# Six more warm-up matmuls on TensorE ahead of a fused attention, FFT-filter and gate kernel

## The chip, the cores and the metric

The kernel runs on one core of one Trainium2 chip. The metric is the device time of one execution in microseconds (us). The kernel before takes 237.54 us (median of three runs, 237.5 to 238.29). Two times are compared as after / before.

A core has five engines that run side by side: TensorE (PE, matmuls; its weight loads are shown apart as PEld), VectorE (DVE), ScalarE (ACT), GpSimd (POOL), and SyncE (SP), which here issues nearly all the transfers (DMAs). Matmuls write into PSUM, which has eight banks here, and another engine copies the result out.

## The reference: what is computed

Three results on the same input `x` of 2048 tokens x 640, in bf16:

```
a = attention with 32 heads of 20, in 4 segments of 512 tokens,
    plus a linear memory (M, z) carried from segment to segment, then @ wo
b = irfft2( rfft2(x) * (w_r + 1j*w_i) )
g = sigmoid( sum(x * gate_w) )
out = g * a + (1 - g) * b
```

Within a segment, q, k and v are `x @ wq`, `x @ wk` and `x @ wv`; the scores are masked with a causal mask and go through a softmax; the memory is read with `phi(q)` and updated with `phi(k)`. What is changed below computes nothing of this: it works on zeros, and nothing reads its result.

## The kernel before, in words

**A recorded program and a planner.** The class `Kern` doesn't write instructions directly. Its methods (`warm_up`, `loads`, `consts`, `project`, `attend`, `fft` and so on, called from `record`, line 860) record operations, each with the buffers that it reads and writes, a planned cost, and the engines that could run it. A group of matmuls is one operation (`mms`, line 544); its planned cost is the sum over its matmuls of `max(columns / 2.4 + 2.8, 25.4)` ns in the mode that the warm-up uses (lines 499 and 547), and it notes two instructions for each matmul, a weight load and the matmul (`op.count`, line 564).

**The order is written out by hand.** `ORDER` (line 633) lists every operation as 2 x its number plus the choice of engine. `Sched.schedule` (line 117) turns it into one queue for each engine and then plays the queues forward in planned time. In that play it settles what is left open:

- which PSUM bank a group of matmuls gets: the one among the allowed ones that comes free first in planned time (`place`, line 159). Groups of the pool "gen" share banks 4 to 7, the scores have 0 to 3;
- which semaphore a transfer gets, and which earlier transfer it must wait for, so that no more than about 1.6 MB is under way (`window`, line 169);
[...]
- when TensorE's code is expected to be there, in blocks of 256 instructions (lines 199 to 203 and 240 to 248).

`emit` (line 290) then writes the waits and the instructions.

**The start.** VectorE clears a tile `G` (line 852), and ten groups of one matmul each multiply zeros into one bank of the pool "gen" (`warm_up`, line 847; `NWARM`, line 858). Each has a 128 x 128 weight and 512 columns and is entered with 1000 columns for the planned cost. They stand first in TensorE's queue. Meanwhile SyncE and ScalarE issue the loads: the first columns of `wq` and `wk`, three transposing loads of the first segment of `x` into `xT` (`xt_load`, line 923), then parts of `xsb` (the same `x` in the order that the FFT wants), the rest of `wk`, `beta`, `fcat` (a table), `wv`, and the rest of `wq`.

**What follows on TensorE.** `proj_direct` (line 1017) computes q and k of the first eight heads straight into the padded layout `qkp`: twenty groups, each four column tiles of 32 wide, which need `xT` and the first columns of `wq` and `wk`. ScalarE and VectorE copy the four results out of PSUM (line 573 on VectorE, 571 on ScalarE), the first scores start from them, and the exponentials (line 1319) start from the scores. Then come the other tiles of k (`proj_tile`, line 1083, which need the rest of `wk`), the first transforms of the FFT on `xsb` once VectorE and GpSimd have folded it (`fold`, line 946), the tiles of v, and the other tiles of q. The projected q and k of the other heads go through a buffer `qk_scr` in the chip's memory and come back as `qkp`. From there on attention, memory and FFT run interleaved to the end.

In the trace all matmuls have line 561 (559 where a weight is split in four), so they are told apart by their tiles; the warm-up's are `psum<-G`.

Of the kernel before, what the change touches and what calls it, by code (L numbers as in the profile page):

```python
# [12 lines left out]
P = 128  # L13
# [5 lines left out]
L = 512  # L19
# [485 lines left out]
class Kern:  # L505
# [10 lines left out]
    def b(self, *key):  # L516
        v = self.bufs.get(key)
        if v is None:
            v = self.bufs[key] = Buf(str(key))
        return v  # L520
# [326 lines left out]
    def warm_up(self):  # L847

        self.Sc.group += 1
        b = self.b  # L850
        t = self.G
        self.one("dve", lambda e: e.memset(t.ap(0, [1, 640]), 0.0), 320, [], [b("warm")], -2.0, name="warm")
        bank = Bank(1, "gen")
        for k in range(self.NWARM):
            self.mms([(lambda k=k: (self.ps(bank, 0, [1, L]), t.ap(0, [1, P]), t.ap(P, [1, L]), True, True, {}), 1000)],
                     [b("warm"), bank], [], -1.0, name="warm")

    NWARM = 10

# [804 lines left out]
```

## Time and profile before

| what | value |
|---|---|
| median of three runs | 237.54 us (237.5 to 238.29) |
| the profiled execution: span from the first to the last instruction | 238.5 us |
| the profiled execution's own time outside the span | not shown; the span is all that is known of it |
| instructions | 10359 |
| busy: PE / DVE / ACT / POOL | 224.9 / 194.8 / 197.1 / 162.0 us |
| the same as shares of the span | 94% / 82% / 83% / 68% |
| mean granted TensorE clock | 0.993 |
| busy share of PE in the windows 0 to 13.5 us and 13.5 to 40 us | 10.23 of 13.50, 26.23 of 26.50 us |

How to read it: a row of the timeline has a start, a duration, an engine, a line of the kernel, and what is written from what; in square brackets stands how long the engine was idle before, and what released it ("issue" when nothing in the profile explains it). Ends of matmuls are modelled, so starts are the safer reading: the distance between the starts of two matmuls of one kind is the pace. The granted clock is a fraction of TensorE's full clock. A chain is the work followed back from the last instruction, at each step to what released it.

### The profile page before, as it was taken

The page shows a single profiled execution, that of the slowest core. Times are in us where ns is not written, and L with a number is a line of the kernel's source. Part 1 is how long each engine was busy: PE and PEld are TensorE (multiplying, and loading weights), DVE is VectorE, ACT ScalarE, POOL GpSimd, SP SyncE. Part 2 cuts the span into 40 slices and gives each one's busy share as a digit, 9 for nine tenths or more (in the row PEclk, how much of TensorE's full clock was granted, in tenths as well). Part 3 has the DMA queues.
Part 4 walks back from the last instruction along what each step waited for, and adds up shares of the span by engine and source line. Part 5 has one row for each costly group of instructions (what it writes and reads, how often), then busy time and mean ns, then how long its engine had stood idle before and what let it go on. Part 6 is the DMA issues. An engine that isn't in the chain of part 4 may idle for free.

```text
span 238.5 us, 10359 instructions
## 1 busy us (share of the span) xinstructions
PE 224.9 (94%) x4391; PEld 142.1 (60%) x4391; DVE 194.8 (82%) x486; ACT 197.1 (83%) x233; POOL 162.0 (68%) x300
## 2 busy tenths in 40 slices
PE   6899999979999999999989999899999999989994
PEld 2576566656546666555657665456554456657794
DVE  0189998859999998899998888999999996847453
ACT  2079888969999998999989999988999888788820
POOL 8133139436769976737888979777998677786840
PEclk9799999999999999999999999999999999999999
DMA  7999659997879586493886683544998767492224
GB/s 148 294 330 271 196 148 171 231 230 157 230 181 231 156 214 184 122 269 100 179 230 186 182 278 87 174 124 138 200 273 210 187 142 109 95 82 85 74 70 110
DMA packets 59121, 42.18 MB, mean 177 GB/s; under 512 B 30212, under 2 KB 55364, under 8 KB 59076
## 3 DMA queue, kind: packets, MB, share of 16 engines
q1 hardware_dynamic: 58036, 40.96, 71.8%
q8 instruction: 34, 0.56, 1.0%
q10 hardware_dynamic: 1040, 0.57, 0.9%
q14 instruction: 11, 0.09, 0.1%
HBM read 23.32 MB, written 12.30 MB: 149 GB/s over the span
## 4 chain that ended last, share of the span: by engine, by line
PE 62%; ACT 13%; DMA 11%; DVE 9%; issue 2%; POOL 1%; SPq 1%; DVEq 0%; POOLq 0%
PE psum L561 54%; ACT ex L1319 11%; PE psum L559 8%; DMA qkp<-qk_scr 3%; DVE Pt L1496 2%; DMA u_scr<-ub 2%; DMA pkn<-phk 2%; DMA xT<-in_A_x_dram 2%; DMA tt<-tab_tt 2%; POOL ex L1340 1%; DMA dnc<-u_scr 1%; DVE qu L573 1%; SPq L594 1%; DVE Bt L573 1%; DVE phk L1141 1%
## 5 line engine op out<-in xcount | busy, mean ns | idle before, releaser
L1319 ACT ACTIVATE ex<-psum 128x2048 bf16<-128x2048 f32 (+4 forms) x92 | 138.5, 1506 | 13.2 <-PE psum L561 10.9
L1340 POOL TENSOR_SCALAR_AFFINE_SELECT ex<-ex 128x256 bf16<-128x256 bf16 (+2 forms) x224 | 118.6, 551 | 29.5 <-ACT ex L1319 6.1
L561 PE MATMUL psum<-qkp 20*64 20x64 bf16 (+5 forms) x1280 | 32.3, 270 | 3.5 <-ACT ex L1319 2.8
L561 PE MATMUL psum<-xT,wq 128*128 128x512 bf16 (+1 forms) x135 | 31.7, 423 | 2.3 <-DMA xT<-in_A_x_dram 2.0
L561 PE MATMUL psum<-xT,wk 128*128 128x256 bf16 (+1 forms) x280 | 32.6, 282 | 1.3 <-issue 1.3
L561 PEld LDWEIGHTS psum<-qkp 20*64 20x64 bf16 x1280 | 13.3, 103 | 21.9 <-ACT ex L1319 16.3
L1496 DVE TENSOR_TENSOR Pt<-psum,Wt 128x642 bf16<-128x642 f32 x32 | 25.4, 818 | 1.1 <-PE psum L561 0.9
L561 PE MATMUL psum<-wv,xT 128*32 128x321 bf16 (+3 forms) x390 | 26.1, 301 | 0.0
L561 PEld LDWEIGHTS psum<-xT,wk 128*128 128x128 bf16 (+1 forms) x280 | 20.5, 101 | 7.8 <-issue 4.0
L961 POOL TENSOR_TENSOR xsb<-xf 128x320 bf16<-128x320 bf16 (+2 forms) x11 | 8.1, 744 | 20.5 <-DVE xf L956 11.3
L559 PE MATMUL psum<-wo,oU 128*32 128x320 bf16 x480 | 21.5, 300 | 0.0
L573 DVE CAST ot<-psum 128x320 bf16<-128x320 f32 x22 | 10.4, 488 | 10.3 <-PE psum L559 7.2
L1171 DVE TENSOR_TENSOR va<-psum,ebx 128x320 bf16<-128x320 f32 x32 | 15.2, 487 | 4.2 <-PE psum L561 2.7
L561 PE MATMUL psum<-big,Cp 128*128 128x321 bf16 (+1 forms) x96 | 18.0, 302 | 0.2
L561 PEld LDWEIGHTS psum<-wv,xT 128*32 128x32 bf16 (+1 forms) x390 | 14.1, 96 | 6.3 <-issue 0.9
L561 PE MATMUL psum<-ex,va 128*32 128x64 bf16 (+3 forms) x576 | 17.6, 257 | 0.2
L561 PE MATMUL psum<-big,Ac 128*128 128x161 bf16 (+2 forms) x96 | 17.8, 256 | 0.0
L573 DVE CAST Bt<-psum 128x322 bf16<-128x322 f32 x28 | 14.3, 520 | 2.5 <-PE psum L561 2.3
L561 PEld LDWEIGHTS psum<-ex,va 128*32 128x32 bf16 x576 | 10.9, 96 | 8.7 <-POOL ex L1340 1.8
L561 PE MATMUL psum<-tt,Yt 128*128 128x256 bf16 (+1 forms) x96 | 15.8, 275 | 0.3 <-DVE Yt L1501 0.3
L1542 DVE TENSOR_TENSOR G<-eo,psum 128x320 bf16<-128x320 f32 x32 | 14.9, 477 | 1.2 <-ACT eo L571 0.5
L561 PEld LDWEIGHTS psum<-xT,wq 128*128 128x128 bf16 (+1 forms) x135 | 9.8, 105 | 10.2 <-DMA xT<-in_A_x_dram 2.5
(98 smaller groups left out, 392.0 us busy)
## 6 DMA issues: line engine op xcount, KB each, us to landing
qkp<-qk_scr SPq DMA_DIRECT2D x28, 160.0 KB
tt<-tab_tt SPq DMA_DIRECT2D x8, 512.0 KB, 4.5
qk_scr<-qu SPq DMA_DIRECT2D x12, 256.0 KB, 2.8
u_scr<-ub SPq DMA_DIRECT2D x12, 256.0 KB, 3.1
xsb<-in_A_x_dram SPq DMA_DIRECT2D x8, 320.0 KB, 5.0
oU<-u_scr SPq DMA_DIRECT2D x15, 128.0 KB, 3.6
out_dram<-ot SPq DMA_DIRECT2D x12, 160.0 KB
Wt<-in_B_w_r_dram SPq DMA_DIRECT2D x16, 80.2 KB, 4.7
```

The lines of the kernel that those rows point to most:

```text
L559: h = e.matmul(dst, wt, r_, start=st, stop=sp_, **{**kw, "tile_position": (0, q), "skip_group_check": True})
L561: h = e.matmul(o_, l_, r_, start=st, stop=sp_, **kw)
L573: alts["dve"] = (lambda e: e.tensor_copy(dst(), src()), 67 + 1.04 * n, 68.0)
L594: return e.dma_start_transpose(d_, s_)
L961: self.either(lambda e, dst=dst, src=src, d0=d0, n=n, op=op: e.tensor_tensor(xs.ap(o + dst, [D, 2], [1, n]), xf.ap(src + d0, [321, 2], [1, ...
L1141: fmin = lambda e: e.tensor_tensor(dst(), dst(), et.ap(0, [1, L]), ALU.min)
L1171: self.one("dve", lambda e: e.tensor_tensor(va.ap(i * H * VW + h0 * VW, [VW, nh], [1, DH]), self.ps(bank, 0, [DH, nh], [1, DH]), self.ebx. ...
L1319: self.one("act", lambda e, d=d, q=q: e.activation(self.ex.ap(*d), self.ps(bank, *q), ACT.Exp, scale=SC), n, [bank], [self.exb(s, 2 * pr + ...
L1340: self.one("pool", lambda e: e.affine_select(self.ex.ap(e0 + d0, [1280, 4], [1, n], np_=np_), self.ex.ap(e0 + s0, [1280, 4], [1, n], np_=np_),
L1496: self.one("dve", lambda e, ri=ri, Pt=Pt, Wt=Wt, wo_=wo_, bank=bank: e.tensor_tensor(Pt.ap(ri * 322, [644, 2], [1, KD]), self.ps(bank, 0, ...
L1542: self.one("dve", lambda e, q=q, n2=n2, bank=bank, eo=eo: e.tensor_tensor(self.G.ap(n2 * D + 639 * q, [1 - 2 * q, 320]), eo.ap(q, [1, 320] ...
```

## The change

Groups 0 to 3 of the ten warm-up groups keep their one matmul. Groups 4 to 9 hold the same matmul twice. So TensorE gets 16 instead of 10 matmuls on zeros, all into the same bank. The number of operations stays the same, and so the numbers in `ORDER` still fit. The planned cost of a doubled group is twice that of a single one, and its count of instructions is 4 instead of 2, so the planner plays the rest of the program from a later planned time of TensorE.

```diff
         for k in range(self.NWARM):
-            self.mms([(lambda k=k: (self.ps(bank, 0, [1, L]), t.ap(0, [1, P]), t.ap(P, [1, L]), True, True, {}), 1000)],
-                     [b("warm"), bank], [], -1.0, name="warm")
+            warm = lambda: (self.ps(bank, 0, [1, L]), t.ap(0, [1, P]), t.ap(P, [1, L]), True, True, {})
+            self.mms([(warm, 1000)] * (1 if k < 4 else 2), [b("warm"), bank], [], -1.0, name="warm")
```

## The prediction

> **What bounds the kernel now.** I read the page first: how busy each engine is, the forty slices, and the chain that ended last. Then came the pieces of that chain in order of time, the busy time by stretches, and the timeline of the first 14 us. On the page:
> ```profile
> span 238.5 us, 10359 instructions
> ...
> PEclk9799999999999999999999999999999999999999
> ...
> PE 62%; ACT 13%; DMA 11%; DVE 9%; issue 2%; POOL 1%; SPq 1%; DVEq 0%; POOLq 0%
> ```
> TensorE carries 62% of the chain. In the second slice (6 to 12 us) the granted clock reads 0.7, the only low place in the whole row. The warm-up sits just ahead of it. The chain of the first 60 us:
> ```profile
> 6.94 29.51 PE psum L561 x425
> ...
> 37.86 0.69 DVE Ac L573
> ...
> 39.69 6.23 DMA qkp<-qk_scr
> ...
> 45.96 4.84 PE psum L561 x113
> 50.80 1.30 issue
> ```
> From 6.94 on TensorE is the chain for 29.5 us without a break, so what TensorE saves early there, the chain saves. Now the clock, in stretches of 3.41 us (why 3.41, below), and two short stretches at its edges:
> ```profile
> 0.63:4.04 3.41, 2.74 (x7) 1.00 0.62 145
> 4.04:7.45 3.41, 1.44 (x21) 1.00 1.12 206
> 7.45:10.87 3.42, 3.42 (x48) 0.50 0.94 307
> ...
> 48.41:51.82 3.41, 2.40 (x55) 1.00 1.11 228
> ```
> ```profile
> 7.40:7.60 0.20, 0.20 (x12) 0.64 0.49 141
> ...
> 10.80:11.00 0.20, 0.20 (x12) 0.83 1.19 365
> ```
> Columns: length, TensorE's busy time (matmuls), granted clock, DMA share, GB/s. A mean of 0.64 in 7.40 to 7.60 puts the drop to one half at 7.46; a mean of 0.83 in 10.80 to 11.00 puts the return at 10.87. The drop lasts 3.41 us. I therefore cut the time into stretches of that length, ending at those two edges. The stretch ahead of the drop was busy 1.44 of 3.41 us (42%). The stretch ahead of the return was full. The one ending at 51.82 was busy 70% and lost nothing.
>
> The matmuls show both clocks:
> ```profile
> L561 PE MATMUL psum<-G x10: 379/620/634, 1.3 to 4.6; 128*128 128x512 bf16 x10
> ```
> ```profile
> 1.30 3.67 PE L561 MATMUL psum<-G 128*128 128x512 bf16 x10 [1.30 <-DVE G L852]
> 6.94 0.40 PE L561 MATMUL psum<-xT,wq 128*32 128x512 bf16 x4 [1.97 <-DMA xT<-in_A_x_dram]
> 7.16 0.39 PE L561 MATMUL psum<-xT,wk 128*32 128x256 bf16 x8
> 7.73 0.66 PE L561 MATMUL psum<-xT,wk 128*32 128x256 bf16 x8
> 8.16 1.08 PE L561 MATMUL psum<-xT,wq 128*32 128x512 bf16 x8
> ...
> 13.08 0.43 PE L561 MATMUL psum<-qkp 20*64 20x512 bf16 x12
> 13.44 3.23 PE L561 MATMUL psum<-xT,wk 128*128 128x256 bf16 x28
> ```
> Groups of real work start 0.22 us apart at 6.94 and 7.16, then 0.43 apart at 7.73 and 8.16: half speed. The ten warm-up matmuls end at 4.97, and 1.97 us of idleness follow. Most of the warm-up went at half speed too, although the clock column reads 1.00 there (nothing is recorded before the first change). Its weight loads show it:
> ```profile
> 3.83 0.15 PEld L561 LDWEIGHTS psum<-G 128*128 128x128 bf16 x1 [0.28 <-issue]
> 4.16 0.31 PEld L561 LDWEIGHTS psum<-G 128*128 128x128 bf16 x2 [0.17 <-issue]
> ```
> Ten matmuls from 1.30 with the last start at 4.6 are 0.37 us apart in the mean, but the loads at 3.83 and 4.16 only 0.33, and the two at 4.16 closer still; so the clock rose near 4.04, the end of a stretch that was busy 2.74 of 3.41 us (80%).
>
> **The change, part by part.** Against the profiled execution: its span is 238.5 us, which is 0.96 above the median of the runs (237.54) and 0.21 above the highest (238.29). Its own time outside the span isn't shown, so I take differences from the span and apply them to the median.
>
> *Six more matmuls.* A full-clock matmul of 512 columns costs, by this row,
> ```profile
> 22.42 3.84 PE L561 MATMUL psum<-xT,wq 128*128 128x512 bf16 x17
> ```
> (3.84 - 0.38) / 16 = 0.216 us, the 0.38 being the tail of the last. Six cost 1.30 us and end at 4.97 + 1.30 = 6.27, ahead of 6.94, where the load xT releases the first real matmul. They cost nothing while the load covers them. Without a rise of the clock at 4.04 they would start 0.43 us apart as at 7.73 and 8.16, take 2.6 us, end at 7.5, and delay the real work by 0.6.
>
> *The clock.* The stretch from 4.04 to 7.45 gets 1.44 + 1.30 = 2.74 us of work, 80%: exactly the share at which the first stretch raised the clock, and above the 70% that kept it. So I expect no drop. Between 7.46 and 10.87 TensorE was full at half clock, and 3.41 x 0.5 = **1.71 us** go.
>
> [...]
>
> *What is late next.* Three things.
> ```profile
> 9.67 1.03 DVE L956 TENSOR_TENSOR xf<-xsb 128x640 bf16<-128x640 bf16 x2 [8.43 <-DMA xsb<-in_A_x_dram]
> 11.73 0.38 SPq L596 DMA_DIRECT2D wq<-in_A_wq_dram  x1
> 12.11 1.94 DVE L573 CAST qkp<-psum 128x512 bf16<-128x512 f32 x3 [1.41 <-PE psum L561]
> 13.07 0.16 PEld L561 LDWEIGHTS psum<-qkp 20*64 20x64 bf16 x12 [0.42 <-DVE qkp L573]
> ```
> ```profile
> SPq L596 <- DMA wk<-in_A_wk_dram: 1.6, 1, 1.6
> ```
> (1) VectorE's first cast would be wanted at 12.11 - 1.71 = 10.40, but two folds hold that engine until 10.70; the first scores behind it then come 0 to 0.3 us later than their 11.37; I take 0.1, since the first of three casts still ends at 10.70 + 0.65 = 11.35. (2) SyncE's issue at 11.73 waited 1.6 us for the second part of wk, so that part landed at about 11.7; the first tile that needs it would start at 13.44 - 1.71 + 0.1 = 11.83, with 0.1 to spare: 0. (3) From there to 37.86 the chain is TensorE, and then VectorE, SyncE, and the 6.23 us of a load. All of them follow TensorE, but stages of the remaining 200 us can give some back. Bounds: loss 0 to 1.6; I take 0.2, because the rows that I have of the next 25 us are of TensorE, not of loads.
>
> *The plan.* The queues keep their written order. But the planner charges each matmul 1000 columns, 1000 / 2.4 + 2.8 = 419.5 ns, so its warm-up is 6 x 0.42 = 2.5 us longer, while the chip's is 1.30 longer and hidden. PSUM banks, semaphores and the waits between VectorE and GpSimd are chosen from these planned times, and some will differ. The nearest row for a badly placed bank:
> ```profile
> PEld psum L561 <- ACT ex L1319: 16.6, 50, 0.9
> ```
> 0.33 us each. I bound this between two such waits fewer (-0.7) and ten more (+3.3), and take 0: the relative order of releases is mostly kept when all of TensorE moves together.
>
> *The code.* Twelve more instructions (a load and a matmul for each) move everything behind them in TensorE's stream. The 1.30 us "issue" at 50.80 stands at
> ```profile
> 0.00:50.81 50.81, 47.01 (x726) 0.97 0.94 222
> ```
> 726 matmuls and as many weight loads; no other engine holds it there, so I read it as code not yet there. Twelve instructions earlier means six matmuls earlier, about 0.9 us of work moved behind the stall. Bounds: -1.30 (it goes) to +0.9; I take 0, as work only changes sides.
>
> **Sum**: -1.71 + 0.1 + 0 + 0.2 + 0 + 0 = -1.4; 237.54 - 1.4 = **236.1 us**.
>
> **The rivals.**
>
> *The drop isn't there in most runs.* The edges at 4.04, 7.46 and 10.87 are those of one execution. If the stretches lie elsewhere against the start, the gap of 1.97 us is shared between two of them. It lies wholly in one in (3.41 - 1.97) / 3.41 = 42% of positions; with a limit as high as the 70% that kept the clock, any stretch with 1.02 us of it would drop, nearly all positions. For it: the span is above all three times, and the runs spread by 0.79 us. Against it: the 0.79 is less than half of a 1.71 us loss that came and went. Then nothing goes: **237.5** (237.1 to 237.9). [...]
>
> *The gain is taken up.* The second part of wk, the folds' loads, or the code at 50.80 come no earlier than now. If the code lands at 52.10 as before, the wait there grows from 1.30 to 2.7 us. For it: DMA shares of 0.94 to 1.12 in the rows from 4 to 14 us, and wk's margin of 0.1. Against it: fetches and most later loads are asked for by work that moves too. Between none and all of 1.4 left: **236.9** (236.4 to 237.5).
>
> *Slower: banks of a mistimed plan.* A group put on the bank that the plan thinks free first, when the chip frees another first, holds all of TensorE's queue. Five waits of 0.33 us eat the gain; from there it is slower; ten give 237.54 - 1.4 + 3.3 = **239.4** (238.3 to 240). For it: the plan's warm-up grows by 2.5 us, and the chip's by 1.30 behind a load. Against it: four banks in an order that is fixed leave few choices.
>
> **How the numbers follow.** Forecast 0.43 (235.5 to 236.5), drop not there 0.22, taken up 0.19, slower 0.16. About 0.5%, 1.2 us, is what a measurement of this kernel can tell from no change. Below 236.35 lies nearly all of the forecast: 0.40. Above 238.73 lies most of the last rival: 0.14. Within: 0.46. The range from 235.5 to 238.6 leaves out that rival's upper part and the case of nothing lost together with a code stall gone. The forecast's own range is 235.5 to 236.5.
>
> **What would show it.** In the changed profile: sixteen matmuls into the warm-up's bank, ending near 6.3; idleness before the first real one of about 0.7; no 0.50 in the clock between 7 and 11, and groups 0.22 us apart throughout; the first scores near 11.4 instead of 13.08; the chain's unbroken piece of TensorE ending near 36.3. A drop that merely moves would refute the share of 80% as the reason. A gain at 13 us that is gone by 53 is the second rival. New waits of TensorE for casts or activations, in number, are the third. A time within 0.3 of 237.5 with a clean clock would say that the runs never had the drop.

## The result: slower by about 1%

| | before | after |
|---|---|---|
| median of four runs beside each other | 237.91 us (237.5 to 238.3) | 241.76 us (240.15 to 242.28) |
| the profiled execution: span | 238.5 us | 240.5 us |
| mean granted clock in it | 0.993 | 1.000 |

After / before is **1.0113**, with a 95% interval of 1.0065 to 1.0161. It was measured again among the experiments (`e8_after_again`): 1.0127 (1.0067 to 1.0187). So the change is slower by 1.1 to 1.3%, some 2.7 to 3.0 us, where 1.4 us faster was forecast. A ratio isn't the quotient of the two medians (1.0162 here). The ratios here and below leave out every execution more than 1.5% above the fastest of its kernel, eight of twelve in e3 and six of twelve in e7, so they understate an edit that makes long executions more frequent. The executions of one kernel spread by 2 to 3%, and many comparisons of this study stand only just clear of that.

A time is about 1.8 us longer than its span (242.27 beside 240.5 for the changed kernel). So the profiled execution of before, with its span of 238.5, took about 240.3, well above the runs that it was to stand for.

The page of the changed kernel:

```profile
span 240.5 us, 10369 instructions
...
PEclk9999999999999999999999999999999999999999
...
PE 57%; ACT 15%; DVE 12%; DMA 6%; SPq 3%; issue 3%; POOL 3%; DVEq 0%; POOLq 0%
```

The low place in the clock is gone, as the change would have it. TensorE carries less of the chain than in the profile that the prediction rests on (57% for 62%), but it does so in the second profile of before as well (56%), which comes next. The first 12 us on TensorE, and the stretches of the clock that the prediction cut (length, TensorE's busy time, granted clock, DMA share, GB/s):

```profile
1.30 6.42 PE L561 MATMUL psum<-G 128*128 128x512 bf16 x16 [1.30 <-DVE G L852]
7.65 0.40 PE L561 MATMUL psum<-xT,wq 128*32 128x512 bf16 x4
7.88 0.39 PE L561 MATMUL psum<-xT,wk 128*32 128x256 bf16 x8
...
12.11 0.43 PE L561 MATMUL psum<-qkp 20*64 20x512 bf16 x12
```

```profile
4.04:7.45 3.41, 3.41 (x11) 1.00 1.11 190
7.45:10.87 3.42, 3.42 (x90) 1.00 1.02 297
```

Sixteen warm-up matmuls take 6.42 us, 0.40 each, so nearly all of them went at half clock. The clock column reads 1.00 there too, but the trace's record of the clock begins only with the rise, at 6.99 in the changed kernel and at 4.04 in the first profile of before. The real work starts behind them without a gap, its groups about 0.22 us apart: full clock from there. What this is worth depends on what it is compared with. The kernel before was profiled once more (`e11_before_again`; 238.50 us, where the median of before in those runs is 238.37), and there it starts like this:

```profile
1.30 4.23 PE L561 MATMUL psum<-G 128*128 128x512 bf16 x10 [1.30 <-DVE G L852]
6.98 0.40 PE L561 MATMUL psum<-xT,wq 128*32 128x512 bf16 x4 [1.45 <-DMA xT<-in_A_x_dram]
7.21 0.39 PE L561 MATMUL psum<-xT,wk 128*32 128x256 bf16 x8
...
11.63 0.43 PE L561 MATMUL psum<-qkp 20*64 20x512 bf16 x12
```

Here too the groups stand 0.22 us apart, after a gap in front of them: this execution has no drop. Its first scores start at 11.63, half a microsecond ahead of the changed kernel's. Only the execution on which the prediction rests has them at 13.08.

From here on, e11 is the execution that the changed kernel is compared with. Its span is 236.7, so 3.8 us have to be found, a little more than the typical loss. The waits of TensorE, first of e11, then of the changed kernel (what was waited for, us in total, times, longest):

```profile
PE psum L561 <- DMA xT<-in_A_x_dram: 1.4, 1, 1.4
...
PE psum L561 <- issue: 1.1, 1, 1.1
PE psum L561 <- DMA qkp<-qk_scr: 1.0, 1, 1.0
...
PE psum L561 <- DVE ot L573: 0.2, 1, 0.2
```

```profile
PE psum L561 <- issue: 1.8, 1, 1.8
...
PE psum L561 <- DVE ot L573: 1.2, 1, 1.2
PE psum L561 <- DMA qkp<-qk_scr: 1.1, 2, 0.9
PE psum L561 <- POOL ex L1340: 1.1, 1, 1.1
PE psum L561 <- DVE Bt L573: 0.9, 1, 0.9
```

The wait for `xT` is gone, because the warm-up now outlasts the load. In its place stand a longer "issue" (+0.7), a wait for GpSimd (+1.1), one for a cast of `Bt` (+0.9) and a longer one for `ot` (+1.0). The chain of the changed kernel shows where two of them lie:

```profile
45.59 4.36 PE psum L561 x107
49.95 1.85 issue
51.80 4.27 PE psum L561 x52
...
60.00 0.34 DVE phk L1141
...
60.41 0.48 POOL Mz L1417
60.90 0.36 POOL ebg L1047
61.25 0.84 POOL ex L1340 x2
62.15 0.61 POOL ex L1340
...
62.88 0.67 POOL ex L1340
63.60 24.85 PE psum L561 x401
```

TensorE's matmuls on `ex` (the exponentials) start at 63.60, right behind the last mask (line 1340) that GpSimd puts on `ex`; GpSimd itself had waited for VectorE's `phk` at 60.00. GpSimd's own rows around that, in e11 and then in the changed kernel:

```profile
59.05 1.73 POOL L1340 TENSOR_SCALAR_AFFINE_SELECT ex<-ex 128x256 bf16<-128x256 bf16 x3 [1.00 <-ACT ex L1319]
```

```profile
58.93 0.66 POOL L1340 TENSOR_SCALAR_AFFINE_SELECT ex<-ex 64x512 bf16<-64x512 bf16 x1 [2.10 <-DVE phk L1140]
60.41 0.48 POOL L1417 TENSOR_TENSOR Mz<-Macc,hm 128x154 bf16<-128x154 f32 x1 [0.83 <-DVE phk L1141]
```

In e11 the masks follow ScalarE's exponentials. In the changed kernel GpSimd stands idle for 2.10 and 0.83 us until VectorE has done its two operations on `phk`. Those are waits that the planner writes (lines 252 to 255): in its play the two engines now come to that place in the other order. Played through, the plan of the change has three such waits here that the plan of before hasn't.

The wait for `ot` is followed up with e7. Taking the lag of the same TensorE instruction behind e11, the 3.8 us add up like this: 0.5 at the first scores (12.11 against 11.63); 0.8 more at the issue stall near 50 (1.85 against 1.08); 1.1 at the mask; 0.9 at `Bt` near 100; 1.2 at `ot` near 213; and about 0.7 given back in between, in places that are too small to tell apart.

### The profile page after: what moved, and what is told of

It is laid out like the page before. It is cut to its first block, busy times and chain, and to the rows that moved or that the text cites. A ratio compares the mean times of both kernels' runs of the same rounds, so it can differ in the third digit from the quotient of the medians.

```text
span 240.5 us, 10369 instructions
## 1 busy us (share of the span) xinstructions
PE 225.8 (94%) x4397; PEld 142.4 (59%) x4397; DVE 194.6 (81%) x486; ACT 196.7 (82%) x233; POOL 161.7 (67%) x300
## 4 chain that ended last, share of the span: by engine, by line
PE 57%; ACT 15%; DVE 12%; DMA 6%; SPq 3%; issue 3%; POOL 3%; DVEq 0%; POOLq 0%
PE psum L561 52%; ACT ex L1319 13%; PE psum L559 5%; DMA qkp<-qk_scr 3%; DVE Pt L1496 3%; SPq L596 3%; POOL ex L1340 2%; DMA out_dram<-ot 2%; DMA dnc<-u_scr 1%; DVE Bt L573 1%; DVE phk L1141 1%; ACT eo L571 1%; DVE va L1171 1%; DVE qu L573 1%; DVE Yt L1501 1%
## 5 line engine op out<-in xcount | busy, mean ns | idle before, releaser
L561 PE MATMUL psum<-xT,wq 128*128 128x512 bf16 (+1 forms) x135 | 30.4, 380 | 0.9 <-DVE Bt L573 0.9
L1128 ACT ACTIVATE et<-qu 128x512 bf16<-128x512 bf16 x25 | 15.3, 624 | 1.3 <-DVE phk L1141 1.2
```

The lines of the kernel that those rows point to most:

```text
L561: h = e.matmul(o_, l_, r_, start=st, stop=sp_, **kw)
L1128: self.one("act", lambda e: e.activation(et.ap(0, [1, L]), qsl(), ACT.Exp), L, [qb], [b("et", pi_)], late, fix=95, name="phi_exp")
```

## The experiments

Two theories stand against each other at first. They have letters in the expectations that follow. **P**, the plan: the planner charges more for the doubled groups, plays the rest differently, and writes other waits. **W**, the matmuls themselves and the instructions that they bring, with an unchanged plan: the work at the start, and the place of the rest in TensorE's code. After e1 to e4, W was split: **C** says that the place of the code costs at a few sensitive points, in whatever direction the borders of the loaded blocks move; **G**, that each added instruction costs. Kernels that ran together shared a chip and the runs of before: e1 to e4, e5 to e8, and e9 to e11.

### e1: sixteen matmuls, the plan of ten

```diff
+            op = self.mms([(warm, 1000)] * (1 if k < 4 else 2), [b("warm"), bank], [], -1.0, name="warm")
+            if k >= 4:
+                f, cost, late = op.alts["pe"]
+                op.alts["pe"], op.count = (f, 1000 * PECOL + 2.8, late), 2
```

The doubled groups are entered with the cost and count of a single one, so every wait, bank and semaphore is that of before.

> Sixteen warm-up matmuls as in the change, but the planner is told the cost and the count of ten, so that banks, waits and transfers are planned exactly as before. Theory P (the loss comes from the plan, above all from three waits of GpSimd for VectorE near 60 us that the longer planned warm-up brings): 236.8 to 238.6, no loss beyond the late start of up to 0.7 us that the profile after shows. Theory W (the loss comes from the matmuls themselves, which end at 7.6 instead of 5.0, and from the code that they shift by twelve instructions): 240 to 242, as the change.

Measured: 241.95 us median beside 239.36, ratio 1.0103 (1.0034 to 1.0173). P alone falls: without any change of the plan the loss is there. At the start the sixteen matmuls take 5.85 us and the first real group comes at 7.73, 0.75 behind e11's. The loss that remains at the end is in part in the same place as in the changed kernel (TensorE waits 1.0 us for `ot` near 213) and in part in another; among TensorE's waits is

```profile
PE psum L561 <- DMA pkn<-phk: 1.5, 1, 1.5
```

a wait near 78 us for `pkn`, a transposing load that neither e11 nor the changed kernel waits for.

### e2: ten matmuls, the plan of sixteen

```diff
+            if k >= 4:
+                f, cost, late = op.alts["pe"]
+                op.alts["pe"], op.count = (f, 2 * cost, late), 4
```

> Ten warm-up matmuls as before, but the planner is told the cost and the count of sixteen, so that banks, waits and transfers are planned exactly as in the change. Theory P: 239.5 to 241.8, and the new wait of TensorE for GpSimd (1.1 us in the profile after, near 63 us) is there again. Theory W: 237.5 to 238.5, as before.

Measured: 240.87 beside 239.36, ratio 1.0102 (1.0045 to 1.016). So W alone falls as well: the chip gets the same matmuls as before and is slower by as much. The wait for the mask is there with its 1.1 us (in this kernel the line is 1343):

```profile
63.60 0.73 PE L561 MATMUL psum<-ex,va 128*32 128x512 bf16 x24 [1.07 <-POOL ex L1340]
```

```profile
62.90 0.73 PE L561 MATMUL psum<-ex,va 128*32 128x512 bf16 x24 [1.07 <-POOL ex L1343]
```

The first row is the changed kernel's, the second e2's: the same gap of 1.07 us at the same matmuls. e2 has no other new wait of that size, and its profiled span is 237.8, 1.1 above e11's. That is less than half of the 1.0% (2.4 us) by the ratio; the profiled execution is the fastest of e2's six, and where the others lose more isn't shown.

### e3 and e4: more and less warm-up, with the plan of before

e3 doubles only groups 7 to 9 (thirteen matmuls), with the cost and count of single ones as in e1. e4 leaves all ten matmuls in their place and cuts six to 8 columns, so neither the plan nor the code moves and only the work shrinks.

```diff
+            op = self.mms([(warm, 1000)] * (1 if k < 7 else 2), [b("warm"), bank], [], -1.0, name="warm")
```

```diff
-... self.ps(bank, 0, [1, L]) ... t.ap(P, [1, L]) ...
+... self.ps(bank, 0, [1, L if k < 4 else 8]) ... t.ap(P, [1, L if k < 4 else 8]) ...
```

> Thirteen warm-up matmuls, planner told of ten. At half clock throughout, thirteen end at about 1.3 + 13 x 0.427 + 0.2 = 7.0, when the first real data land, so they can't delay the start by more than 0.1 us. Theory P: 236.8 to 238.0, at or a little under the kernel before. Theory W: half of the change's loss, about 239.5.

> Six of the ten warm-up matmuls are cut from 512 to 8 columns, planner told of ten as before; the result is the same. The real work then starts at half clock in nearly every execution and stays there until up to 3.4 us later. If an early loss is carried to the end: 1.0 to 1.7 us more than before, 238.9 to 239.6. If it is absorbed by loads: within 0.4 us of before. Theories P and W give no difference here; the run gives the price of the clock.

Measured: e3 242.54 (237.85 to 244.85 in twelve runs), ratio 1.004 (0.9974 to 1.0105), which tells nothing from no change and rests on four executions; 7 of its 12 executions have a mean clock of 0.993 or less. The profiled one shows where that came from. TensorE waited 2.52 us for `pkn` at 77 to 79.7, and then the clock halved:

```profile
79.72 0.44 PE L561 MATMUL psum<-va,pkn 128*128 128x154 bf16 x4 [2.52 <-DMA pkn<-phk]
```

```profile
80.00:81.00 1.00, 1.00 (x24) 0.86 0.15 51
81.00:82.00 1.00, 0.78 (x5) 0.50 0.17 41
...
84.00:85.00 1.00, 1.00 (x21) 0.93 0.54 190
```

The means put the drop at 80.72 and the return at 84.14: 3.42 us, the length of the drop in the prediction, but from another gap.

e4: 240.19, ratio 1.0036 (0.9994 to 1.0078). With six tiny matmuls the real work begins at half clock, its groups 0.43 apart, and the first scores come 2.2 us behind e11's:

```profile
6.99 0.62 PE L561 MATMUL psum<-xT,wq 128*32 128x512 bf16 x4 [3.66 <-DMA xT<-in_A_x_dram]
7.40 0.64 PE L561 MATMUL psum<-xT,wk 128*32 128x256 bf16 x8
7.82 0.64 PE L561 MATMUL psum<-xT,wq 128*32 128x512 bf16 x4
8.25 0.64 PE L561 MATMUL psum<-xT,wk 128*32 128x256 bf16 x8
...
9.96 1.50 PE L561 MATMUL psum<-xT,wq 128*32 128x512 bf16 x12
11.24 1.38 PE L561 MATMUL psum<-xT,wk 128*32 128x256 bf16 x32
12.44 0.38 PE L561 MATMUL psum<-xT,wq 128*32 128x512 bf16 x4
12.66 0.82 PE L561 MATMUL psum<-xT,wk 128*32 128x256 bf16 x24
...
13.84 0.43 PE L561 MATMUL psum<-qkp 20*64 20x512 bf16 x12
```

The three groups from 9.96 to 11.24 still stand 0.43 apart, those at 12.44 and 12.66 0.22: half clock lasts over 4 us from 6.99, where up to 3.4 was expected.

Yet the whole kernel loses 0.36% of 239.4, 0.9 us (between nothing and 1.9 by the interval). So early time seems worth less than itself at the end, by the middle value under half. That speaks against the gain that the prediction carried through (1.4 of 1.6), but it doesn't settle it. In single executions most of an early loss stays for long: by the lag of the same TensorE instructions behind e11, 1.4 of e4's 2.2 us are still there at 90 us, and 1.0 of the 1.45 that the first profile of before lost by the drop (13.08 against 11.63).

### e5 and e6: the GpSimd waits taken out of the change, and put into before

e5 is the change, with three VectorE operations held back in the planner's play until the GpSimd operations that go ahead of them in before have been played. e6 is the kernel before, with the three GpSimd operations that wait in the changed plan waiting here too.

```diff
+            first = {1002: 1119, 1003: 307, 501: 313}.get(o.id)
+            if first is not None and ops[first].t1 is None:
+                return None
```

```diff
+            first = {332: 1002, 400: 1003, 313: 501}.get(o.id)
+            if first is not None:
+                if ops[first].t1 is None:
+                    return None
+                t = max(t, ops[first].t1 + 35.0)
...
+                if o.id in (332, 400, 313):
+                    o.dyn.append(ops[{332: 1002, 400: 1003, 313: 501}[o.id]])
```

> The change, but in the planner's play three VectorE operations (two maxima and minima of phi, one addition on the weights) are held until the GpSimd operations that went ahead of them in the plan before have been placed; so the new waits of GpSimd for VectorE near 60 us are gone, and the rest of the change's plan stays. Theory P: TensorE's 1.1 us wait for GpSimd near 62 us is gone from the profile, and the time is about 1.1 us under the change's in this call. Theory W: the wait is worth nothing in the end; the time is the change's within 0.5.

> The kernel before with nothing of the change but those three waits: the three GpSimd operations wait for the three VectorE operations, as in the change. Theory P: a wait of TensorE for GpSimd of about 1.1 us near 62 us, and 1.1 us more than before, 0.4 to 0.5%. Theory W: no difference in time.

Measured: e6 239.59 beside 238.46, ratio **1.0084** (1.0042 to 1.0126). Three waits of GpSimd for VectorE, and nothing else (every bank stays as it was, and so does every wait elsewhere), make the kernel before slower by most of what the whole plan costs, and the 1.07 us gap stands in its trace at the same matmuls. So that part of P is shown. The 0.84% are 2.0 us (1.0 to 3.0), more than the gap; the profile has one more wait that e11 hasn't, 1.5 us for a cast of `Cp` near 108, and no run shows whether it comes from the three.

e5: 240.4 beside 238.46, six runs from 235.79 to 242.2, which spread too far for a ratio. By time it is inconclusive; its trace isn't. The wait for the mask is gone, and another has come:

```profile
PE psum L564 <- DMA pkn<-phk: 2.0, 1, 2.0
```

In the changed kernel TensorE comes to `pkn` later, because of the mask among other things, and finds it there. Take the mask's wait away, and `pkn` is what it waits for: here the two don't add. In e5 the load itself also takes longer, 7.2 us from issue to landing for 4.4, and behind the wait the clock stands at 0.50 for 3.41 us.

### e7, e9, e10: the code moved, with nothing else

Ten full matmuls as before, and 6, 12 or 32 further ones of 8 columns (12, 24 and 64 instructions), with the plan of ten. The tiny ones are meant to cost nearly no time: in e7 all sixteen take 4.58 us, where ten full ones take 4.23 in e11 and 4.45 in e2. The edit of e7; e9 has `[(tiny, 1000)] * (0 if k < 4 else 2)` behind `[(warm, 1000)]`, e10 `* (0 if k < 2 else 4)`:

```diff
+            tiny = lambda: (self.ps(bank, 0, [1, 8]), t.ap(0, [1, P]), t.ap(P, [1, 8]), True, True, {})
+            op = self.mms([(warm, 1000), (tiny, 1000)][:1 if k < 4 else 2], [b("warm"), bank], [], -1.0, name="warm")
```

> Ten warm-up matmuls of 512 columns as before, and six more of only 8 columns, planner told of ten: the plan and, within 0.2 us, the warm-up's length are as before, while all later instructions of TensorE stand twelve places later in its code, as in the change. Theory W in the form that the shifted code is to blame (code loads then fall together with other issues of SyncE, as at 67 us in the run with sixteen hidden matmuls, where an issue took 2.2 instead of 1.3 us): 1 to 2 us more than before. Theory P: as before, within 0.5 us.

> As the run with the code shift alone, but with twelve tiny matmuls of 8 columns instead of six: everything behind stands 24 instead of 12 places later, the plan is as before. Theory C (where the blocks of TensorE's code fall against the transfers decides how late the transposed load pkn lands that TensorE needs at 78 us; after 12 places it took 7.4 us from issue to landing instead of 4.8): the landing differs again, and the time with it, between 237.5 and 241.5 in no order with the size of the shift. Theory G (any more instructions on TensorE cost time, by their number): twice the loss of the shift by 12, about 242 to 244.

> The same with 32 tiny matmuls, 64 places. Theory C: anything between 237.5 and 241.5, with the lateness of pkn at 78 us going along with the time. Theory G: over 245.

Measured: e7 241.18 beside 238.46, ratio **1.0084** (1.0028 to 1.014). e9 242.77 beside 238.37, 1.0196 (1.0151 to 1.0242). e10 243.28 beside 238.37, 1.0219 (1.0177 to 1.0262). It isn't the work at the start that costs: the first scores of e7 and e9 start at 11.61 and 11.38, those of e11 at 11.63. e10's start late, at 13.24, but its TensorE is 0.7 ahead of e11's from 51 to 77 us. The place of TensorE's code alone makes the kernel slower. (In these runs, as in e1 and e3, the planner isn't told where the code now stands; in the changed kernel it is.) It isn't G in its plain form: from 12 to 24 instructions 1.1% come on top, from 24 to 64 only 0.2%. It isn't C as stated either, which allowed no more than 241.5 for e9 and e10: all three shifts tried are slower, none faster. Three shifts can't say whether the place of before is a lucky one.

Where the profiled execution of e7 loses can be read in its chain, its waits, and SyncE's issues:

```profile
72.76 7.40 DMA pkn<-phk
```

```profile
PE psum L561 <- DMA pkn<-phk: 2.7, 1, 2.7
...
PE psum L561 <- DVE ot L573: 1.4, 1, 1.4
```

```profile
66.57 2.62 SPq L594 DMA_TRANSPOSE xT<-in_A_x_dram  x1
...
207.74 2.24 SPq L594 DMA_TRANSPOSE mT<-o_scr  x1
```

The same two issues in e11, and the one of `mT` in the changed kernel with the store behind it and TensorE's row that follows:

```profile
65.97 1.30 SPq L594 DMA_TRANSPOSE xT<-in_A_x_dram  x1
...
203.46 1.24 SPq L594 DMA_TRANSPOSE mT<-o_scr  x1
204.76 0.55 SPq L596 DMA_DIRECT2D out_dram<-ot  x1
```

```profile
206.39 2.11 SPq L594 DMA_TRANSPOSE mT<-o_scr  x1
208.55 0.55 SPq L596 DMA_DIRECT2D out_dram<-ot  x1
```

```profile
213.60 0.32 PE L561 MATMUL psum<-G,fbg 128*32 128x320 bf16 x4 [1.23 <-DVE ot L573]
```

An issue of a transposing load takes about 1.3 us, and 2.1 to 2.6 in these places. What falls together with it is one packet of 16384 bytes on the queue that the profile's page calls "q8 instruction". There are 34 of them in a run (35 in e10), for 4397 matmuls and 4397 weight loads in the changed kernel, 259 to a packet. The planner counts TensorE's code in blocks of 256 (lines 199 to 203), so the packets are read as blocks of that code. The records of the packets against those of the `mT` issue that stands ahead of this store (us):

| kernel | instructions added | `mT` issue starts | block's packet starts | that is later by | issue takes |
|---|---|---|---|---|---|
| e11 | 0 | 203.46 | 204.84 | 1.38 | 1.24 |
| before | 0 | 204.91 | 206.00 | 1.09 | 1.24 |
| e2 | 0 | 204.90 | 205.68 | 0.78 | 1.24 |
| e4 | 0 | 206.22 | 206.97 | 0.75 | 1.25 |
| e6 | 0 | 205.04 | 205.90 | 0.86 | 1.24 |
| e3 | 6 | 208.52 | 209.36 | 0.84 | 1.24 |
| changed | 12 | 206.39 | 206.93 | 0.54 | 2.11 |
| e8 | 12 | 206.09 | 206.73 | 0.64 | 2.32 |
| e1 | 12 | 206.47 | 207.01 | 0.54 | 1.90 |
| e5 | 12 | 205.80 | 206.35 | 0.55 | 1.87 |
| e7 | 12 | 207.74 | 208.34 | 0.60 | 2.24 |
| e9 | 24 | 206.34 | 207.37 | 1.03 | 1.24 |
| e10 | 64 | 207.36 | 207.84 | 0.48 | 1.88 |

Where the packet starts within 0.64 us of the issue's start, the issue is stretched, in six kernels of six; where it starts 0.75 us or more behind it, it isn't, in seven of seven. It depends on the place and not on the number of instructions, and that much is C. Stretched issues as such aren't new: e11 has them too, in places where no wait of TensorE over 0.4 us follows, for example

```profile
104.37 2.08 SPq L594 DMA_TRANSPOSE pkn<-phk  x1
...
111.17 2.62 SPq L594 DMA_TRANSPOSE pkn<-phk  x1
```

and its next issue of `mT`, behind the store, takes 1.63 us where the changed kernel's takes 1.20. What the shift changes is which issues a block meets. The way from there to TensorE: the store of `ot` is queued on SyncE behind `mT`. In the changed kernel `mT` is issued 2.93 us later than in e11 and the store 3.79 later (208.55 against 204.76); the 0.87 us of longer issue go to the store, to the cast that needs `ot` free, and to TensorE. The cast's row in the changed kernel:

```profile
213.06 0.49 DVE L573 CAST ot<-psum 128x320 bf16<-128x320 f32 x1 [1.78 <-DMA out_dram<-ot]
```

What isn't settled: why `pkn` takes 7.40 us from issue to landing in e7 (4.4 in the changed kernel, 5.6 in e11). The stretched `xT` ahead of it doesn't explain it: in e3, e5 and e10 that issue takes 1.3 us, and `pkn` still 6.8, 7.2 and 6.6. Nor is it shown that `pkn` makes up e7's 0.84%. Its profiled execution took 243.79 beside a median of 241.18; behind the wait of 2.7 us the clock stood at 0.50 for 3.42 us, as in e3, which adds 1.6 us of lag; and 7 of e7's 12 executions have a mean clock of 0.993 or less, five of which the ratio leaves out. For e9 the profiled execution was the fastest of its six and the only one with a mean clock of 1.000 (the others have 0.986 to 0.995), so drops of the clock are probably a part of its 2%. What that execution shows against e11 is 0.8 us at a load of `qkp` near 38, 1.3 at `Bt` near 100 and 0.8 near 109; neither `pkn` nor `ot` is among them. e10 loses at the start (1.6, still at half clock until 10 us), gets that back by 51 us, and loses at the end (TensorE waits 1.3 us for VectorE's line 1546 and 1.1 for `ot`).

### e8 and e11: the two kernels again

Both without an edit.

> The change itself, to be compared with the others of this call on one chip, since single executions of one kernel spread by over 2%. Both theories: 2 to 3.5 us over before; a new wait for GpSimd of about 1.1 us near 62 us whatever the clock did at the start.

> The kernel before, profiled once more beside the others of this call. If the drop of the clock at 7.5 us in its first profile belongs to the position of the clock's stretches in that one execution, the start looks different here: ten warm-up matmuls at half clock ending at 5.7, no drop, first scores near 11.5; and no wait over 0.5 us for GpSimd at 62 us or for pkn at 78 us. If the drop belongs to the kernel, it is there again, with the first scores near 13.1.

Measured: e8 240.26 beside 238.46, ratio 1.0127 (1.0067 to 1.0187), with the mask's wait of 1.1 us, the `mT` issue at 2.32 and TensorE's wait for `ot` at 1.5. In it the issue stall near 50 us is not longer than in e11, and it has no wait for `Bt` near 100; it lost 0.7 at the load of `qkp` near 38 instead. So the mask and `ot` are there in both executions of the change, and the 0.8 and 0.9 us at the other two places in one only (a wait for `Bt` near 100 is in e4 and e9 too). e11 239.2 beside 238.37, ratio 1.0026 (0.9989 to 1.0063): two series of one kernel differ by that much.

No version that beats the kernel before came out of these runs.

## Why the prediction was wrong

- **The base: the step that failed first.** The prediction took 1.71 us off for a drop of the clock that it saw in one execution, and applied the difference to the median of others. A mean clock of 0.993 or less, as such a drop gives it (3.41 x 0.5 / 238.5 = 0.007), is in 17 of the 63 executions of before that ran beside the experiments, and in 2 of e11's 12. Where in those executions it lay isn't on record; five others with ten full matmuls that were profiled (e2, e6, e7, e9, e11) have none at the start. A drop of 1.71 us that is there about one time in four is worth at most 0.5 us in the mean, and little in the median. This is the first rival, and it was right about the start. The profile had said so: a span above all three times. "Less than half of a 1.71 us loss that came and went" was no argument, since three runs can miss what comes one time in four.
- **The clock, as a mechanism: right in its outcome, untested in its reason.** Sixteen matmuls, no 0.50 between 7 and 11, groups 0.22 apart; no drop there in any of the profiled executions with sixteen full matmuls (the changed kernel, e1, e8). But the stretch from 4.04 to 7.45 was busy for 3.41 of 3.41 us and not for 2.74, because the warm-up went on at half clock until no gap was left. So the share of 80% wasn't put to the test, and since most executions don't have the drop, there was little to cure.
- **Six more matmuls at 0: right only under its condition.** It named 0.6 us for the case that the clock doesn't rise at 4.04. The case came: 7.65 and 7.73 for the first real group against 6.98, 0.7 late. The warm-up ends at 7.72, 1.45 us later than the 6.27 forecast.
- **What is late next, +0.3: probably too small.** By the middle value e4 keeps 0.9 of 2.2 us to the end, by its interval between nothing and 1.9. The second rival may be right here as well, but there was little gain to take up.
- **The code at 50.80: right in kind.** The stall came six matmuls earlier; work changes sides. The block's packet ahead of it moved with the work, from 49.39 in before to 48.87. Its size varies between executions (1.85 us in the changed kernel, under 0.7 in e8, beside 1.08 in e11), within the bound of +0.9.
- **The code, as a whole, at 0 (-1.30 to +0.9): the size and the place failed.** The prediction looked only at the stall where TensorE itself waits for code. e7 gives +0.84%, 2.0 us (0.7 to 3.3), for the same twelve instructions. In its profile the loss is at `ot` behind the stretched issue of `mT` near 206, which the changed kernel shares, and at `pkn` near 78, which it doesn't; what share each has in the 2.0 us stays open.
- **The plan at 0 (-0.7 to +3.3): the value failed, the bound held.** e2 gives +1.0% and e6 +0.84%. Most of it needs no change of the banks, which the slower rival priced: e6 leaves every bank as it was. It is in the waits between VectorE and GpSimd, which the prediction named in one clause and gave no row: one gap of 1.07 us on TensorE, and the rest not located. The slower rival had the right sign and the wrong mechanism; its 239.4 was 2.4 below what came.
- **The sum.** Plan and code are about 1.0 and 0.8% alone and 1.1 to 1.3% together. That they don't add fits e5, where a TensorE that isn't held up by the mask waits for `pkn`; the intervals alone would allow a plain sum. Against this stands no gain that the runs can show: e1, with the matmuls, is at 1.0103, and e7, with their code alone, at 1.0084.

## What to carry to other kernels

Ahead of a gain that is read from one execution, ask whether its span fits the times of the others; a clock drop that is in some executions of one kernel and not in others (here a mean clock of 0.993 or less in 17 of 63) must be counted over many. In a kernel whose order, waits and code are fixed to the last microsecond, work that is put in front of an engine's queue isn't free because a load covers it: price the plan that is computed from it and the code that moves behind it, by running each alone (the cost hidden from the planner; the instructions without their work). And look at the transfers' issuing engine as well as at the one whose code moves.

## What the runs showed of the hardware

- **The clock rose at different times in the profiled executions.** Ten identical matmuls from 1.30 take 3.67 us in the first profile, 4.23 in e11 and 4.45 in e2, sixteen take 6.42 in the changed kernel and 5.85 in e1: the rise comes earlier or later. The drops last 3.41 us (before, e5) and 3.42 (e3, e7). Four gaps of TensorE were followed by one: 1.97 us (before), 2.52 (e3), 2.74 (e7) and 1.99 (e5). Gaps of up to 1.85 us (the changed kernel, near 50) were followed by none; the 3.66 us in e4 lie at its start, with groups 0.43 apart behind them.
- **Where a block of code arrives, another engine's issue takes longer.** SyncE's issue of `mT` ahead of the store takes 1.24 or 1.25 us in seven executions, and 1.87 (e5) to 2.32 (e8) in the six in which a block's packet starts 0.48 to 0.64 us behind the issue's start. e7's issue of `xT` at 66.57, with a packet between 66 and 68 us, takes 2.62. Besides these issues, TensorE itself stands for 1.08 us in e11 and 1.85 in the changed kernel near 50 us. In eleven of the thirteen profiled executions there is such a stall behind the 724th to 726th recorded matmul, and it ends 1.36 to 1.71 us after the end of a block's packet.
